# The first six pairs' steps in another order, with GpSimd at work from the first load on

## The chip, the cores and the metric

One Trainium2 chip, one of its cores. The metric is device time in microseconds (us) of one execution. The kernel before took 942.79 us (median of 3 runs, 941.56 to 943.15). The profile comes from one more execution of 941.53 us, whose instructions span 939.8 us. A difference of under 0.2% (about 1.9 us) can't be told from none here.

## The reference

Attention over 8 batches of 8 heads (576 tokens, 64 wide, rotated queries and keys, softmax), whose result goes through a layer of 8 experts, of which each token takes the best one. Cut to what matters:

```python
def rotate(x):
    x1, x2 = (x[..., :half], x[..., half:])
    return np.concatenate([x1 * cos - x2 * sin, x1 * sin + x2 * cos], axis=-1)
q_rot, k_rot = (rotate(q), rotate(k))
scores = scale * np.matmul(q_rot, k_rot.transpose(0, 1, 3, 2))
scores = scores - np.max(scores, axis=-1, keepdims=True)
attn = np.exp(scores)
attn = attn / (np.sum(attn, axis=-1, keepdims=True) + 1e-09)
x = np.matmul(attn, v)            # then, for each token, the expert with the largest logit:
h = np.maximum(xe @ w1[e], 0.0)
out[mask] = gate_w[mask, None] * (h @ w2[e])
```

## The kernel before

The 64 heads are worked on as 32 **pairs** (0 to 31), two heads at a time; the experts follow from about 475 us on. All that the change touches lies in the first 100 us.

A pair is a chain of **steps**, each with a short name: the middle says what it does, the last letter which engine does it (v VectorE, called DVE in the profile; a ScalarE, ACT; g GpSimd, POOL; p TensorE, PE; d a DMA). The steps of pair n:

- FPd fetches queries and keys to a tile `qk` (two such tiles, so the fetch of pair n waits until pair n-2 has been rotated); VPd fetches values.
- RQa, RQc, RQb rotate Q (two products, one sum; `do_R`, lines 561, 563, 566) and RKa, RKc, RKb do it for K. All six read and write SBUF alone, 128x576 in fp32.
- HQ and HK (`do_H`, line 569) round the result to the upper part of a two-part number, LQ and LK (`do_L`, line 581) compute the lower part. Scores are the three products upper x upper, lower x upper, upper x lower.
- DX and DY (`do_D`, line 586) exchange the halves of Q's upper and lower part in SBUF by DMA, so that both heads can be multiplied at once.
- S0 to S8 are the nine score tiles (PE, line 611), M0 to M8 their row maxima (DVE, line 616, from PSUM), E0 to E8 the exponentials (ACT, line 627). Four double banks of PSUM (`pb`) go round: a score tile needs one that an exponential or a copy has freed.
- TA, TB, TR and T3 transpose the exponentials on PE, and cA, cB, cR and c3 copy them out of PSUM (DVE or ACT, line 569). V0 and V1 multiply by the values (line 700), U0 and U1 copy the result, O turns it back (line 742), RZ and X divide by the sums. WT casts a few constants for the routing (four copies on DVE, lines 785 to 788); FL0 to FL4 fill an index list in DRAM.

The order of all this is written by hand in three tables: `FIRST` for the first pairs, then `PLAN`, a window that repeats, then `LAST`. `listed_steps` walks `FIRST` and performs each entry; `chained_emit` ties every instruction of an engine to the one before it on that engine, so the table's order is each engine's order. DMAs are tied on SP's queue alone. `done` keeps a step from being performed twice, so what `FIRST` has done `PLAN` leaves out. Which engine a step runs on is the last letter in the table.

Ahead of the table stand the loads of pair 0 (`first_loads`: Q's half of the tile first, then K's) and `WARM` small matmuls that keep PE at work until the first scores.

## Time and profile before

| | |
|---|---|
| median of 3 runs | 942.79 us |
| the profiled execution, its span | 941.53 us, 939.8 us |
| PE busy over the span | 921.5 us (98%) |
| DVE, ACT, POOL busy | 748.7, 630.1, 653.4 us |
| granted TensorE clock | 1.00 throughout (the level of 2.4 GHz) |

PE is busy nearly all the time, but "busy" is a span from start to modelled end, so a stall shows as little more than a thinner count of matmuls. The share of one engine over the whole span says nothing on the opening: there one reads the stretches (busy time of each engine from one time to another) and the timeline, in which a row gives start, length, engine, line, operation and tiles, and in brackets how long the engine had been idle and who ended that.

### The profile page before, as it was taken

To read this page: it belongs to the slowest core of one execution; us is meant where nothing else is said; L and a number is where in the kernel's file an instruction comes from. 1 tells how busy PE (TensorE), PEld (TensorE's weight loads), DVE (VectorE), ACT (ScalarE), POOL (GpSimd) and SP (SyncE) were. 2 spreads that over 40 slices of the span, in tenths; PEclk is the share of its full clock that TensorE was granted. 3 is DMA by queue.
4 is the path that set the end of the run, shared out by engine and by line. 5 is a ranking of instruction groups with operands and counts; after the bars stand their busy time and mean duration, and the time that the engine had idled before them with its cause. 6 is when DMAs were issued, how large, how long until landed. Compare 5 with 4: busy or idle time off the path is not lost.

```text
span 939.8 us, 25385 instructions
## 1 busy us (share of the span) xinstructions
PE 921.5 (98%) x9579; PEld 769.7 (82%) x9579; DVE 748.7 (80%) x1305; ACT 630.1 (67%) x1123; POOL 653.4 (70%) x559
## 2 busy tenths in 40 slices
...
GB/s 263 244 255 171 168 165 151 187 180 147 184 175 203 133 209 157 129 167 106 220 75 48 72 225 234 206 51 123 163 56 155 157 51 47 44 168 194 409 352 52
...
## 3 DMA queue, kind: packets, MB, share of 16 engines
...
q8 instruction: 77, 1.26, 0.6%
q14 instruction: 56, 0.45, 0.2%
...
## 4 chain that ended last, share of the span: by engine, by line
issue 21%; POOL 18%; PE 10%; DMA 2%; POOLq 1%; DVE 0%; SPq 0%; ACT 0%; DVEq 0%; ACTq 0%
POOL xg L447 6%; POOL xt L447 6%; PE pb L1184 5%; POOL out_dram L1210 4%; PE pb L1320 3%; POOL xsm L1070 1%; DMA out_dram<-y,gi 1%; POOLq L1253 1%; PE pb L700 1%; DMA r<-in_moe_w_dram 1%; DMA xg<-x_dram,gi 0%; PE pb L1133 0%; POOLq L447 0%; DVE PT L569 0%; POOLq L1210 0%
## 5 line engine op out<-in xcount | busy, mean ns | idle before, releaser
L627 ACT ACTIVATE pn<-pb,negm 128x576 f32<-128x576 f32 x256 | 187.4, 739 | 60.1 <-DVE negm L616 57.6
L616 DVE TENSOR_REDUCE negm<-pb 128x1 f32<-128x576 f32 x288 | 201.3, 746 | 23.2 <-PE pb L611 19.0
L611 PE MATMUL pb<-rK,rX 64*128 64x288 f32 (+1 forms) x960 | 163.9, 307 | 3.4 <-ACT pn L627 0.9
L611 PE MATMUL pb<-rK,rQ 64*128 64x288 f32 (+1 forms) x960 | 163.8, 307 | 2.8 <-DVE PT L569 1.0
L1184 PE MATMUL pb<-xh,w1h 128*128 128x256 f32 x544 | 153.8, 283 | 0.0
L1184 PE MATMUL pb<-xh,w1l 128*128 128x256 f32 x544 | 153.7, 283 | 0.0
L1184 PE MATMUL pb<-xl,w1h 128*128 128x256 f32 x544 | 153.7, 283 | 0.0
L700 PE MATMUL pb<-PT,vn 128*64 128x320 f32 (+1 forms) x1024 | 148.9, 412 | 1.0 <-ACT pn L627 0.5
L611 PEld LDWEIGHTS pb<-rK,rX 64*128 64x128 f32 (+1 forms) x960 | 131.9, 179 | 21.6 <-issue 9.8
L611 PEld LDWEIGHTS pb<-rK,rQ 64*128 64x128 f32 (+1 forms) x960 | 131.6, 179 | 11.3 <-DVE PT L569 7.4
L447 POOL DMA_INDIRECT xg<-x_dram,gp x64 | 91.5, 1430 | 54.7 <-DVE gp L257 38.2
L1089 DVE TENSOR_TENSOR w2l<-r,w2h 128x1024 fp32r<-128x1024 f32 x89 | 107.3, 1216 | 19.5 <-ACT w2h L1088 17.3
L569 ACT COPY PT<-pb 128x1024 f32<-128x1024 f32 (+1 forms) x112 | 101.7, 930 | 26.1 <-PE pb L661 22.1
L447 POOL DMA_INDIRECT xt<-x_dram,gp x56 | 80.8, 1442 | 49.1 <-DVE gp L257 31.7
L700 PEld LDWEIGHTS pb<-PT,vn 128*64 128x64 f32 x1024 | 67.9, 136 | 49.7 <-issue 5.7
L1184 PEld LDWEIGHTS pb<-xh,w1h 128*128 128x128 f32 x544 | 106.1, 195 | 0.7
L1184 PEld LDWEIGHTS pb<-xh,w1l 128*128 128x128 f32 x544 | 106.1, 195 | 0.5
L1089 DVE TENSOR_TENSOR w1l<-r,w1h 128x1024 fp32r<-128x1024 f32 x88 | 104.5, 1219 | 2.2 <-ACT w1h L1088 1.8
L1320 PE MATMUL pb<-w2h,hh 128*128 128x512 f32 x272 | 106.2, 390 | 0.0
L1184 PEld LDWEIGHTS pb<-xl,w1h 128*128 128x128 f32 x544 | 106.1, 195 | 0.0
L1320 PE MATMUL pb<-w2l,hh 128*128 128x512 f32 x272 | 106.0, 390 | 0.0
L1320 PE MATMUL pb<-w2h,hl 128*128 128x512 f32 x272 | 105.9, 389 | 0.0
...
## 6 DMA issues: line engine op xcount, KB each, us to landing
...
rX<-rQ SPq DMA_DIRECT2D x128, 144.0 KB
...
```

Source lines behind the costliest of these rows:

```text
L447: nc.gpsimd.indirect_dma_start(out=t[:, k], out_offset=None, in_=x_dram.rearrange("n (q w) -> (n q) w", q=4), in_offset=bass.IndirectOffse ...
L569: (nc.scalar.copy if eng == "a" else nc.vector.tensor_copy)(out=o, in_=i)
L611: nc.tensor.matmul(sp[0:m, r, 0:HS], lhsT=st["Q" if r == h else "X"][rows[r], a, cols], rhs=parts(st["K"][rows[r], b])[:, h], start=(a + b ...
L616: nc.vector.tensor_reduce(out=st["negm"][:, j:j + 1], in_=st["S", j][:, :, 0:HS], axis=AX.XY, op=ALU.max, negate=True)
L627: nc.scalar.activation(out=parts(pt), in_=sp[:, :, 0:HS], func=AF.Exp, bias=st["negm"][:, j:j + 1], scale=1.0, accum_out=z)
L700: m = nc.tensor.matmul(to[:, 0:w], lhsT=st["vn"][:, h, kt, :], rhs=st["PT"][:, 4 * h + kt, half * 256:half * 256 + w], start=(kt == 0), st ...
L1070: nc.gpsimd.indirect_dma_start(out=xsm[:, j], out_offset=None, in_=x_dram, in_offset=bass.IndirectOffsetOnAxis(ap=sib[:, j:j + 1], axis=0) ...
L1089: nc.vector.tensor_tensor(out=lo, in0=src, in1=hi.bitcast(F32), op=ALU.subtract)
L1184: m = nc.tensor.matmul(hp[:, fi], lhsT=w, rhs=x, start=(i == 0), stop=(i == len(todo) - 1))
L1210: sc = nc.gpsimd.indirect_dma_start(out=out, out_offset=bass.IndirectOffsetOnAxis(ap=si[:, t:t + 1], axis=0), in_=y, in_offset=None, bound ...
L1253: nc.gpsimd.drain()
L1320: m = nc.tensor.matmul(yp[:, t], lhsT=h[:, fi, ts_], rhs=w[:, fi], start=(g == 0 and fi == 0 and i == 0), stop=(g == FQ - 1 and fi == 1 an ...
```

## The change

Three edits. The part of `FIRST` up to pair 6 is written in another order and with other engine letters; from pair 3's gate on (`gBv` 3) every engine's order is as before. `WARM` falls from 195 to 185. In `do_D`, pair 0's first half of each exchange is issued from ACT's queue and not SP's. The first two lines of the table, before and after, and the other edits:

```diff
-    ("RQav", 0), ("FPd", 1), ("RQcv", 0), ("RQbv", 0), ("HQa", 0), ("DXd", 0), ("WIa", 0), ("RKcv", 0), ("LQv", 0),
-    ("DYd", 0), ("RKav", 0), ("RKbv", 0), ("RKav", 1), ("RQav", 1), ("HKa", 0), ("FPd", 2), ("RQag", 2), ("RQcv",
+    ("RKcg", 0), ("FPd", 1), ("RQav", 0), ("RQcv", 0), ("RQbv", 0), ("HQa", 0), ("DXd", 0), ("RKav", 0), ("RQcg",
+    1), ("LQv", 0), ("RKbv", 0), ("HKa", 0), ("WIa", 0), ("RKcv", 1), ("DYd", 0), ("RQav", 1), ("LKv", 0), ("RQbv",
...
-WARM = 195
+WARM = 185
...
         for h in range(2):
-            m = nc.sync.dma_start(out=st["X"].bitcast(F32)[rows[1 - h], a], in_=st["Q"].bitcast(F32)[rows[h], a])
+            q = nc.sync if n or h else nc.scalar
+            m = q.dma_start(out=st["X"].bitcast(F32)[rows[1 - h], a], in_=st["Q"].bitcast(F32)[rows[h], a])
```

**Steps that change engine.** From VectorE to GpSimd: RKc 0, RQc 1, RKa 1, RKc 2. From GpSimd to VectorE: RKc 3, LK 3, RKa 4, RQb 4, RKc 4, LK 4, RQb 5, LK 5. Casts from ScalarE to VectorE: HQ 3, HQ 4, HK 4, HQ 5, HK 7. Copies from VectorE to ScalarE: cA0 2, cA0 3, U0 3, U1 3, cB1 5; the other way: cA1 5. WT moves from pair 4's scores to pair 3's.

**The opening on VectorE.** Before, from the first rotation to the first maximum (`qk_138` is pair 0's tile, `qk_347` pair 1's; `yQ`, `yK` are rotated, `rQ`, `rK` the two-part tiles):

```order
L561 TENSOR_TENSOR qk_138<-qk_138,rotq_112 128x576
L563 TENSOR_TENSOR qk_138<-qk_138,rotq_112 128x576
L566 TENSOR_TENSOR yQ_350<-qk_138 128x576
L563 TENSOR_TENSOR qk_138<-qk_138,rotk_111 128x576
L581 TENSOR_TENSOR rQ_353<-yQ_350,rQ_353 128x576
L561 TENSOR_TENSOR qk_138<-qk_138,rotk_111 128x576
L566 TENSOR_TENSOR yK_365<-qk_138 128x576
L561 TENSOR_TENSOR qk_347<-qk_347,rotk_111 128x576
L561 TENSOR_TENSOR qk_347<-qk_347,rotq_112 128x576
L563 TENSOR_TENSOR qk_347<-qk_347,rotq_112 128x576
L563 TENSOR_TENSOR qk_347<-qk_347,rotk_111 128x576
L566 TENSOR_TENSOR yQ_381<-qk_347 128x576
```

Behind these come LK 0, RKb 1 and the first maximum, so fourteen steps stand ahead of it. Now, to the first maximum (the tiles' numbers are new: `qk_337` is pair 1's):

```order
L561 TENSOR_TENSOR qk_138<-qk_138,rotq_112 128x576
L563 TENSOR_TENSOR qk_138<-qk_138,rotq_112 128x576
L566 TENSOR_TENSOR yQ_341<-qk_138 128x576
L561 TENSOR_TENSOR qk_138<-qk_138,rotk_111 128x576
L581 TENSOR_TENSOR rQ_344<-yQ_341,rQ_344 128x576
L566 TENSOR_TENSOR yK_352<-qk_138 128x576
L563 TENSOR_TENSOR qk_337<-qk_337,rotk_111 128x576
L561 TENSOR_TENSOR qk_337<-qk_337,rotq_112 128x576
L581 TENSOR_TENSOR rK_343<-yK_352,rK_343 128x576
L566 TENSOR_TENSOR yQ_362<-qk_337 128x576
L566 TENSOR_TENSOR yK_381<-qk_337 128x576
L617 TENSOR_REDUCE negm_374<-pb0_104 128x1
```

Eleven steps are left on VectorE. The other three open GpSimd's queue now (the first three rows; the fourth is LQ 1, then pair 2 begins), where before its first step was RQa of pair 2:

```order
L563 TENSOR_TENSOR qk_138<-qk_138,rotk_111 128x576
L563 TENSOR_TENSOR qk_337<-qk_337,rotq_112 128x576
L561 TENSOR_TENSOR qk_337<-qk_337,rotk_111 128x576
L581 TENSOR_TENSOR rQ_366<-yQ_362,rQ_366 128x576
L563 TENSOR_TENSOR qk_369<-qk_369,rotq_112 128x576
```

The sixth and the last row on VectorE, RKb of pairs 0 and 1, need the first and the third of these.

**VectorE in pair 2's scores.** Before, from M0 2 on: maxima, the reciprocal sums of pairs 0 and 2 (RZ), U1 0, two copies.

```order
L616 TENSOR_REDUCE negm_760<-pb2_106 128x1
L734 TENSOR_REDUCE rz_857<-z0_124 128x10
L735 RECIPROCAL rz_857<-rz_857 128x10
L616 TENSOR_REDUCE negm_760<-pb0_104 128x1
L616 TENSOR_REDUCE negm_760<-pb1_105 128x1
L616 TENSOR_REDUCE negm_760<-pb2_106 128x1
L734 TENSOR_REDUCE rz_889<-z2_128 128x10
L735 RECIPROCAL rz_889<-rz_889 128x10
L720 COPY uT0_130<-pb3_107 128x5x64
L569 COPY PT_931<-pb0_104 128x2x2x256
```

Now the same stretch has HQ 3, LK 3, RKa 4, RQb 4, RKc 4 and HQ 4 among the maxima (`qk_715` is pair 4's tile):

```order
L569 CAST rQ_803<-yQ_784 128x576
L617 TENSOR_REDUCE negm_753<-pb2_106 128x1
L735 TENSOR_REDUCE rz_820<-z0_124 128x10
L736 RECIPROCAL rz_820<-rz_820 128x10
L581 TENSOR_TENSOR rK_802<-yK_750,rK_802 128x576
L561 TENSOR_TENSOR qk_715<-qk_715,rotk_111 128x576
L617 TENSOR_REDUCE negm_753<-pb0_104 128x1
L566 TENSOR_TENSOR yQ_871<-qk_715 128x576
L617 TENSOR_REDUCE negm_753<-pb1_105 128x1
L617 TENSOR_REDUCE negm_753<-pb2_106 128x1
L563 TENSOR_TENSOR qk_715<-qk_715,rotk_111 128x576
L721 COPY uT0_130<-pb3_107 128x5x64
```

HQ 4 follows these rows; RKc 3 stands a little ahead of them, among pair 1's copies.

## Rows read from the trace of the kernel before

**Rows 1.** Stretches: from:to, length, busy (instructions) of PE, PEld, DVE, ACT, POOL, clock

```profile
13.37:20.00 6.63, 4.48 (x50) 3.37 (x48) 6.44 (x11) 4.38 (x11) 1.74 (x2) 1.00 0.99 308
20.00:40.00 20.00, 17.19 (x278) 13.55 (x276) 19.21 (x26) 18.81 (x42) 19.45 (x14) 1.00 0.73 221
40.00:60.00 20.00, 19.86 (x260) 14.48 (x260) 14.89 (x28) 16.84 (x40) 19.84 (x16) 1.00 0.87 274
60.00:80.00 20.00, 19.62 (x318) 15.45 (x316) 18.73 (x26) 14.77 (x31) 18.79 (x14) 1.00 0.54 158
200.00:300.00 100.00, 99.53 (x1452) 76.00 (x1450) 81.44 (x151) 78.50 (x169) 90.93 (x81) 1.00 0.62 174
```

**Rows 2.** Timeline of VectorE: first two rotations, and the first maxima

```profile
6.28 0.76 DVE L561 TENSOR_TENSOR qk<-qk,rotq 128x576 f32<-128x576 f32 x1 [5.28 <-DMA qk<-in_qk_dram]
6.95 0.75 DVE L563 TENSOR_TENSOR qk<-qk,rotq 128x576 f32<-128x576 f32 x1
...
11.38 0.75 DVE L561 TENSOR_TENSOR qk<-qk,rotk 128x576 f32<-128x576 f32 x1
...
16.18 3.41 DVE L616 TENSOR_REDUCE negm<-pb 128x1 f32<-128x576 f32 x5
```

**Rows 3.** Timeline of the other engines in the opening

```profile
1.06 12.38 PE L990 MATMUL pb<-onesb 128*128 128x128 bf16 x195 [1.06 <-DVE onesb L224]
...
15.53 0.40 PE L611 MATMUL pb<-rK,rX 64*128 64x288 f32 x1 [0.90 <-DVE rK L581]
...
9.23 3.09 SPq L586 DMA_DIRECT2D rX<-rQ  x4
...
16.96 0.74 ACT L627 ACTIVATE pn<-pb,negm 128x576 f32<-128x576 f32 x1
...
22.70 0.78 ACT L627 ACTIVATE pn<-pb,negm 128x576 f32<-128x576 f32 x1
```

**Rows 4.** Timeline of GpSimd from its first step, and VectorE's one step beside it

```profile
18.26 1.42 POOL L561 TENSOR_TENSOR qk<-qk,rotq 128x576 f32<-128x576 f32 x1 [16.29 <-DVE negm L616]
...
23.88 1.41 POOL L581 TENSOR_TENSOR rK<-yK,rK 128x576 fp32r<-128x576 f32 x1
25.25 1.93 POOL L581 TENSOR_TENSOR rQ<-yQ,rQ 128x576 fp32r<-128x576 f32 x1
...
24.02 1.88 DVE L563 TENSOR_TENSOR qk<-qk,rotk 128x576 f32<-128x576 f32 x1
```

**Rows 5.** Timeline of VectorE: other SBUF steps, and GpSimd beside two of them

```profile
69.13 1.02 DVE L785 CAST tid<-cst 128x640 int32<-128x640 f32 x1
70.07 1.39 DVE L786 COPY run<-cst 128x8 f32<-128x8 f32 x1
...
72.80 2.07 DVE L616 TENSOR_REDUCE negm<-pb 128x1 f32<-128x576 f32 x3
...
69.76 1.67 POOL L566 TENSOR_TENSOR yQ<-qk 128x576 f32<-128x576 f32 x1
...
434.90 0.45 DVE L569 CAST rQ<-yQ 128x576 fp32r<-128x576 f32 x1
```

**Rows 6.** Timeline of VectorE from 35 us: its idle times, and c3 of three pairs

```profile
35.81 1.23 DVE L569 COPY PT<-pb 128x1024 f32<-128x1024 f32 x1 [0.61 <-PE pb L661]
...
43.15 2.09 DVE L616 TENSOR_REDUCE negm<-pb 128x1 f32<-128x576 f32 x3 [1.76 <-PE pb L611]
46.25 0.17 DVE L734 TENSOR_REDUCE rz<-z 128x10 f32<-128x20 f32 x1 [1.01 <-ACT pn L627]
...
51.67 0.46 DVE L569 COPY PT<-pb 64x64 f32<-64x64 f32 x2
...
53.26 0.76 DVE L616 TENSOR_REDUCE negm<-pb 128x1 f32<-128x576 f32 x1
...
65.54 0.46 DVE L569 COPY PT<-pb 64x64 f32<-64x64 f32 x2
...
80.03 0.46 DVE L569 COPY PT<-pb 64x64 f32<-64x64 f32 x2
```

22 lines of the change are left out of this document (7 added, 15 removed), and 68 rows, old and new, of the table FIRST.

## The prediction

> **What bounds the kernel now.** I read the stretches first [rows 1]. From 40 us on TensorE is busy nearly without a break (99.5% of 200 to 300 us), and a pair takes 13.87 us from one c3 to the next (51.67 to 65.54) [rows 6]. Ahead of 40 us it is not: 2.15 us idle of the 6.63 to 20 us, 2.81 us to 40 us, while from 20 to 40 us VectorE is busy for 19.21 us, GpSimd for 19.45 and ScalarE for 18.81 of 20 us. So the opening hangs on the engines that feed TensorE, and what it loses there is never given back, since TensorE bounds what follows. The most that a better order of this stretch can bring is about those 5 us; what a worse one costs has no such limit.
>
> Then I read the opening itself. VectorE rotates two pairs alone, from 6.28 us, when Q has landed, to the first maximum at 16.18 us, 0.67 us from one step to the next [rows 2]. GpSimd begins at 18.26 us [rows 4]. TensorE's warming matmuls end at 13.44 us, its last wait for VectorE's lower part of K at 15.53 us, and nine exponentials begin from 16.96 to 22.70 us, one each 0.72 us [rows 3]. Next I looked for what VectorE and GpSimd do when both work on SBUF, since the change makes them do so all along. At 24.02 us VectorE has its one rotation beside GpSimd, RKc 2: 1.88 us for a step of 0.75 [rows 4]. The reader is to see three ends there: GpSimd's step of 23.88 us ends unhurt at 25.29, VectorE's 0.61 us later at 25.90, and GpSimd's next, which began at 25.25, only at 27.18, 1.28 us after VectorE's. The two did not overlap; they took turns. A copy of eight columns (`run`, 70.07 us) takes 1.39 us in the same way, until GpSimd's step of 69.76 ends, and that step itself is stretched to 1.67 [rows 5]. A cast to fp32r with GpSimd at rest takes 0.45 us.
>
> **The opening, step by step.** The change takes three of fourteen steps ahead of the first maximum from VectorE and gives them to GpSimd, and VectorE needs their results ahead of its sixth, tenth and eleventh. If the two take turns, the time is the sum: 11 x 0.67 = 7.4 us and 3 x 1.28 = 3.8 us behind 6.28 us, which makes the first maximum 17.5 us, 1.3 us later than now. If they worked side by side, GpSimd's second and third step could begin when pair 1 has landed (it has by 11.38 us, when VectorE reads it without a wait [rows 2]) and end 2 x 1.41 us later, at 14.2 us, and RKb 1 would end at 14.9 us: 1.3 us earlier than now. These are the bounds, and I take the first, since RKc 2 at 24.02 us is the same operation beside the same operation.
>
> The other two edits cost and bring nothing in that case. Ten warming matmuls fewer are 10 x 12.38 / 195 = 0.63 us, so TensorE is free at 12.8 us, but the upper part of K is then there only after six steps of VectorE, one or two of GpSimd and a cast: 6.28 + 4.0 + 2.6 + 0.7 = 13.6 us at the later end, and its lower part only after nine and three, 6.28 + 6.0 + 3.8 = 16.1 us, against 15.5 now. The exchange on two queues takes two of four issues of 0.77 us (3.09 / 4 [rows 3]) off SP, so the lower half of Q goes about 1.5 us earlier; the wait for the lower part of K ends after it in either order, so that hides it. On ScalarE's queue the two issues stand ahead of the cast of K. If each holds that engine as long as one holds SP's queue, 0.77 us, the second, which waits for LQ 0 (five steps and one, 6.28 + 3.4 + 1.3 = 11.0 us), is through at 11.8, ahead of that cast, which waits for RKb 0: nothing. Cover gone, it would be 0.8 us.
>
> **VectorE up to pair 0's output.** From its first maximum (16.18 us) to the first one behind pair 0's X (53.26 us) VectorE takes 37.1 us, of which it idles 0.61 + 1.76 + 1.01 = 3.4 us [rows 6]: 33.7 us of work. The change takes RKc 2 with its stall (1.88) and the copy cA0 2 (1.23) away: 30.6. It adds RKc 3, LK 3, RKa 4, RQb 4, RKc 4, 5 x 0.67, and the casts HQ 3 and HQ 4, 2 x 0.45: 34.8 us. That is without a turn waited for. Each of the seven waits between nothing (GpSimd at rest) and 1.28 us. GpSimd is busy for 39.3 of the 40 us from 20 to 60 us now [rows 1], but in the new order it often waits for one of these very steps (LQ 3 for HQ 3, RKb 4 for RKa 4 and RKc 4, LQ 4 for HQ 4), so I take 0.45 us each, a third: 3.1 us. Of the 3.4 us of idling most is filled; I keep 0.8. Sum: 17.5 + 34.8 + 3.1 + 0.8 = 56.2 us against 53.26: **+2.9 us**. What is late next are pair 2's last maxima: exponentials, transposes and so TensorE wait for them, and only four double banks of PSUM lie between.
>
> **The pair behind it.** From c3 of pair 1 to that of pair 2 VectorE now also has WT, which takes from 69.13 to 72.80 us, 3.7 us, for waiting in turn [rows 5]; before, it lay one pair later, and that pair took 14.49 us (65.54 to 80.03) and not 13.87 [rows 6]. The new sum: nine maxima 6.2 (3.41 / 5 each), WT 3.7, LK 4 and RQb 5 1.3, HK 4 and HQ 5 0.9, two copies of U at most 0.9 together (c3, of two small copies, is 0.46), one of PT 1.2, c3 and X 1.6 (51.67 to 53.26): 15.8 us, and turns of some 0.1 us net, since WT's price holds GpSimd fully busy and here it has six steps of 1.41 in that time. I take 15.9: 2.0 over the 13.87 of before, and the pair after it falls from 14.49 to 13.87: **+1.4 us**. Behind that only LK 5 and HK 7 are added, some 2 us in two pairs in which VectorE has to spare (it is busy 81.44 of 100 us later on [rows 1]), and from pair 3's gate on the order is the old one.
>
> **Sum:** +2.9 + 1.4 = +4.3 us on an execution of 941.53 us, 945.8; the median of the runs lies 1.26 us above the profiled one, so 947.1. Ends of this case: with hardly a turn waited for and no idling, 17.5 + 34.8 + 0.5 = 52.8, and WT at 2.5 us, it comes to about 0, which is the first rival; with half a turn for each of the seven and the four steps and 1.5 us of idling, 17.5 + 34.8 + 4.5 + 1.5 - 53.3 = 5.0 and 15.8 + 2.6 - 13.9 - 0.6 = 3.9, so +8.9.
>
> **The rivals.** *The added steps fall into GpSimd's rests.* GpSimd begins 10 us earlier, has four steps fewer up to pair 3's gate, and waits for VectorE at four places. Then only the opening's 1.3 us is lost and RKc 2's stall of 1.1 us is won back: between -1.9 and +1.9 us, about +0.3, 943.1 us. For it: `uT`, maxima and copies from PSUM lie between most of the added steps. Against it: three of them follow each other within two maxima.
>
> *The two engines do work side by side, and the change is faster.* The place is the opening. The first maximum comes at 14.9 us, the exponentials with it, RKc 2 is gone from VectorE, and up to pair 0's output it ends at 14.9 + 34.8 + 1.2 idle = 50.9 us, 2.4 us earlier; WT then lies in a pair that TensorE bounds, 0.6 us more: -3.0 us, 939.8 us. It decides from the point where VectorE's mean wait per rotation beside GpSimd is under about 0.2 us. For it speaks that RKc 2 is a single row of its kind; against it, that its three ends fit taking turns to 0.1 us, and the copies in rows 5. The Trainium skill's page "Advanced Engine Details and Errata" (VectorE Performance Modes, Mode Summary) names blocking by GpSimd only for VectorE's two-port modes, and "VectorE: DVE Perf Modes" has none of those for an fp32 tensor_tensor: by these two alone the rotations would run free and this rival would be the forecast. The row at 24.02 us differs, and "SBUF — State Buffer" (SBUF: two separate sides) has the wider rule, a lock against any step with two SBUF inputs, which the row bears out; so the measurement decides for turns.
>
> *TensorE's clock falls.* It is granted 1.00 in all stretches, through waits to 15.53 us too. In the new opening TensorE stands nearly idle from 12.8 to 16.1 us. An estimate from the warming matmuls, which run at the upper level (2.4 GHz): 128 columns take 0.063 us [rows 3], 288 columns 0.143, and a pair's nine score tiles, 30 double steps, 4.3 us; at the lower level (1.2 GHz) 8.6 us, against 9 x 0.72 = 6.5 us of exponentials, which hide the first and not the second: +2.1 us more. I count it, at one in ten, within the forecast.
>
> That the table is not followed is no rival: the built order has the three steps at the head of GpSimd's queue.
>
> **How the numbers follow.** Under 0.2% (1.9 us) can't be told from none. The forecast (turns, VectorE late in pairs 2 and 3, +1.9 to +9 us) 0.58; the rests 0.21; side by side 0.21. So slower 0.58, same 0.21, faster 0.21. The range leaves about a tenth on either side: 940.0 takes in half of the faster case, 951.5 most of the turns.
>
> **What would show it.** Right: in the opening VectorE's rotations from the fourth on alternate between 0.75 and some 2 us, the first maximum stands at 17.5 us, SBUF steps among pair 2's maxima take over 1 us each, TensorE's count of matmuls from 40 to 60 us falls, and c3 of pair 1 comes some 3 us later. Wrong: rotations of 0.75 us beside GpSimd's of 1.41, a first maximum ahead of 16 us, and c3 of pair 2 ahead of 65 us.

## The result and the profile after

The changed kernel is slower: 951.67 us (median of 4 runs, 951.09 to 952.16) against 942.96 for the kernel before beside it (941.56 to 943.15), a ratio of 1.0095, 95% interval 1.0078 to 1.0113. That is +8.7 us; +4.3 were forecast, with a range to 951.5 us. The profiled execution took 951.09 us (span 949.3), 9.6 us more than the profiled one of before. Behind the first edits the lines of the code are one higher than before.

The opening, VectorE's timeline and GpSimd's (start, length, engine, line, operation, tiles, and in brackets the idle time ahead and who ended it); it answers to [rows 2] and [rows 4]:

```profile
6.19 0.76 DVE L561 TENSOR_TENSOR qk<-qk,rotq 128x576 f32<-128x576 f32 x1 [5.19 <-DMA qk<-in_qk_dram]
...
8.32 1.96 DVE L561 TENSOR_TENSOR qk<-qk,rotk 128x576 f32<-128x576 f32 x1
10.21 0.75 DVE L581 TENSOR_TENSOR rQ<-yQ,rQ 128x576 fp32r<-128x576 f32 x1
10.88 1.96 DVE L566 TENSOR_TENSOR yK<-qk 128x576 f32<-128x576 f32 x1
12.75 1.96 DVE L563 TENSOR_TENSOR qk<-qk,rotk 128x576 f32<-128x576 f32 x1
...
17.31 2.08 DVE L617 TENSOR_REDUCE negm<-pb 128x1 f32<-128x576 f32 x3
```

```profile
7.78 1.89 POOL L563 TENSOR_TENSOR qk<-qk,rotk 128x576 f32<-128x576 f32 x1 [5.80 <-DMA qk<-in_qk_dram]
10.67 1.55 POOL L563 TENSOR_TENSOR qk<-qk,rotq 128x576 f32<-128x576 f32 x1 [1.00 <-DMA qk<-in_qk_dram]
12.18 1.92 POOL L561 TENSOR_TENSOR qk<-qk,rotk 128x576 f32<-128x576 f32 x1
```

Three of VectorE's rotations take 1.96 us and the others 0.75, each of the three beside one of GpSimd's three steps. The engines take turns, and the first maximum comes at 17.31 us (16.18 before).

The stretches, which answer to [rows 1] (from:to, length, busy time and instructions of PE, PEld, DVE, ACT, POOL, then the granted clock):

```profile
20.00:40.00 20.00, 17.80 (x288) 14.14 (x284) 18.61 (x27) 18.84 (x44) 18.68 (x14) 1.00 0.96 247
40.00:60.00 20.00, 17.78 (x228) 13.77 (x228) 19.48 (x30) 13.25 (x30) 12.35 (x9) 0.91 0.68 196
48.00:50.00 2.00, 0.71 (x16) 0.58 (x16) 2.00 (x4) 0.83 (x3) 0.00 (x0) 1.00 0.56 167
50.00:52.00 2.00, 1.69 (x40) 1.55 (x40) 2.00 (x3) 2.00 (x6) 1.39 (x1) 0.86 0.00 0
52.00:54.00 2.00, 2.00 (x26) 2.00 (x26) 1.97 (x5) 1.79 (x2) 1.55 (x3) 0.50 0.27 58
54.00:56.00 2.00, 2.00 (x34) 2.00 (x32) 1.81 (x3) 1.54 (x5) 2.00 (x2) 0.79 0.88 176
470.00:480.00 10.00, 8.15 (x76) 5.40 (x72) 3.54 (x5) 3.21 (x7) 6.17 (x3) 0.83 0.80 290
```

From 40 to 60 us VectorE is busy for 19.48 us, where it was for 14.89, and GpSimd for 12.35, where it was for 19.84: the work has gone from one to the other. TensorE is busy for 0.71 of the 2 us from 48 to 50 us, and behind that its granted clock falls from 1.00 to 0.50 (the level of 1.2 GHz) for some 3.4 us: (0.14 + 0.50 + 0.21) x 2 / 0.5. It falls again at 474 us. The first fall hardly sets a time, since VectorE is the late one there; what it idles is 0.41 us, ahead of X (below).

VectorE from the first of its seven added steps to X of pair 0, with pair 2's maxima among them, and ScalarE, which waits for these:

```profile
35.22 1.47 DVE L563 TENSOR_TENSOR qk<-qk,rotk 128x576 f32<-128x576 f32 x1
...
41.07 1.34 DVE L569 CAST rQ<-yQ 128x576 fp32r<-128x576 f32 x1
...
43.32 1.25 DVE L581 TENSOR_TENSOR rK<-yK,rK 128x576 fp32r<-128x576 f32 x1
44.49 1.96 DVE L561 TENSOR_TENSOR qk<-qk,rotk 128x576 f32<-128x576 f32 x1
46.38 0.74 DVE L617 TENSOR_REDUCE negm<-pb 128x1 f32<-128x576 f32 x1
47.04 1.43 DVE L566 TENSOR_TENSOR yQ<-qk 128x576 f32<-128x576 f32 x1
48.39 1.41 DVE L617 TENSOR_REDUCE negm<-pb 128x1 f32<-128x576 f32 x2
49.72 0.74 DVE L563 TENSOR_TENSOR qk<-qk,rotk 128x576 f32<-128x576 f32 x1
...
50.79 1.54 DVE L569 CAST rQ<-yQ 128x576 fp32r<-128x576 f32 x1
...
56.22 0.82 DVE L767 TENSOR_TENSOR xt<-pb,rz 128x640 f32<-128x640 f32 x1 [0.41 <-PE pb L674]
56.96 0.23 DVE L769 TENSOR_TENSOR lgt<-pb,rz 128x80 f32<-128x80 f32 x1
```

```profile
47.16 0.74 ACT L628 ACTIVATE pn<-pb,negm 128x576 f32<-128x576 f32 x1 [3.21 <-DVE negm L617]
...
49.17 0.74 ACT L628 ACTIVATE pn<-pb,negm 128x576 f32<-128x576 f32 x1 [1.18 <-DVE negm L617]
```

The row at 56.96 us ends X of pair 0. In the kernel before it is

```profile
52.88 0.23 DVE L768 TENSOR_TENSOR lgt<-pb,rz 128x80 f32<-128x80 f32 x1
```

Such a row stands in every kernel for each of the 32 pairs, and its distance to the same row of the kernel before is called the **lateness** of that pair's X here: +4.1 us for pair 0, +5.1 for pair 1, +5.1 for pair 3, +5.8 for pair 9, +7.2 for pair 29 and +9.6 for pair 30, behind the start of the experts. So half of the loss arises up to X of pair 1, and nearly all of the other half behind pair 3.

### The profile page after: what moved, and what is told of

Read it like the earlier page. It is cut to its first block, busy times and chain, and to the rows that moved or that the text cites. A ratio compares the mean times of both kernels' runs of the same rounds, so it can differ in the third digit from the quotient of the medians.

```text
span 949.3 us, 25373 instructions
## 1 busy us (share of the span) xinstructions
PE 926.8 (98%) x9569; PEld 773.1 (81%) x9569; DVE 756.7 (80%) x1310; ACT 630.3 (66%) x1122; POOL 648.7 (68%) x555
## 4 chain that ended last, share of the span: by engine, by line
PE 42%; issue 21%; POOL 17%; DMA 7%; DVE 7%; ACT 2%; POOLq 1%; SPq 1%; DVEq 0%; ACTq 0%
PE pb L612 10%; PE pb L701 10%; PE pb L1185 7%; PE pb L1321 6%; POOL xg L447 5%; POOL xt L447 4%; PE pb L638 4%; POOL out_dram L1211 4%; DVE PT L569 3%; PE pb L743 3%; PE pb L706 2%; DMA qk<-in_qk_dram 2%; DVE negm L617 1%; ACT pn L628 1%; DMA out_dram<-y,gi 1%
## 5 line engine op out<-in xcount | busy, mean ns | idle before, releaser
L612 PE MATMUL pb<-rK,rX 64*128 64x288 f32 (+1 forms) x960 | 166.2, 309 | 4.7 <-ACT pn L628 1.9
L612 PE MATMUL pb<-rK,rQ 64*128 64x288 f32 (+1 forms) x960 | 166.2, 309 | 3.3 <-DVE lgt L769 1.4
```

What stands on the lines that cost most here:

```text
L612: nc.tensor.matmul(sp[0:m, r, 0:HS], lhsT=st["Q" if r == h else "X"][rows[r], a, cols], rhs=parts(st["K"][rows[r], b])[:, h], start=(a + b ...
```

## The experiments

Medians are in us, each beside the kernel before on the same chip. Lateness is that of the profiled execution, in us.

| kernel | median, before | ratio, 95% interval | X 0 | X 1 | X 3 | X 9 | X 29 | X 30 |
|---|---|---|---|---|---|---|---|---|
| changed kernel | 951.7, 943.0 | 1.0078 to 1.0113 | +4.1 | +5.1 | +5.1 | +5.8 | +7.2 | +9.6 |
| late_start | 947.1, 943.1 | 1.0026 to 1.0054 | +3.7 | +3.7 | +3.3 | +3.5 | +4.3 | +4.7 |
| small_edits | 942.9, 943.1 | 0.9987 to 1.0017 | -1.1 | -1.1 | -1.7 | -2.2 | -1.6 | -1.6 |
| open_on_vector | 952.7, 943.1 | 1.0069 to 1.0130 | +3.9 | +5.7 | +7.0 | +6.9 | +7.6 | +7.7 |
| back_to_gpsimd | 953.6, 943.1 | 1.0070 to 1.0140 | +3.4 | +5.6 | +8.7 | +8.5 | +9.2 | +11.2 |
| changed_again | 949.9, 943.7 | 1.0050 to 1.0099 | +3.3 | +4.5 | +4.8 | +5.2 | +5.8 | +8.2 |
| clock_held | 952.1, 943.7 | 1.0055 to 1.0108 | +4.9 | +8.7 | +8.7 | +9.1 | +10.2 | +10.3 |
| maxima_first | 950.9, 943.7 | 1.0058 to 1.0098 | +2.9 | +4.1 | +6.8 | +7.1 | +7.9 | +8.2 |
| open_shared | 950.4, 943.7 | 1.0056 to 1.0102 | +7.0 | +7.0 | +6.9 | +7.6 | +8.9 | +8.9 |
| new_opening | 943.8, 942.8 | 1.0000 to 1.0020 | +0.7 | +0.7 | +1.2 | +1.7 | +1.7 | +1.5 |
| old_opening | 947.2, 942.8 | 1.0033 to 1.0066 | +3.3 | +4.5 | +7.3 | +7.5 | +8.2 | +8.3 |
| pair4_late | 953.0, 942.8 | 1.0081 to 1.0131 | +2.5 | +4.9 | +6.6 | +9.4 | +10.4 | +10.9 |
| order_alone | 949.1, 942.9 | 1.0029 to 1.0080 | +3.9 | +5.1 | +7.5 | +8.3 | +8.9 | +10.7 |
| engines_alone | 952.8, 942.9 | 1.0069 to 1.0127 | +5.6 | +9.6 | +11.5 | +12.6 | +12.7 | +12.4 |
| hk7_on_scalar | 950.9, 942.9 | 1.0054 to 1.0114 | +2.3 | +6.3 | +6.5 | +8.9 | +9.6 | +11.3 |
| rkc2_on_gpsimd | 942.9, 942.9 | 0.9989 to 1.0019 | +0.8 | +0.8 | +0.2 | +0.3 | +0.3 | +0.3 |
| loads_early | 950.9, 942.9 | 1.0039 to 1.0093 | +2.9 | +7.3 | +7.0 | +7.5 | +8.2 | +12.1 |
| loads_early_changed | 951.1, 942.9 | 1.0047 to 1.0093 | +3.4 | +6.4 | +6.1 | +6.3 | +7.0 | +9.5 |

Single executions of one kernel differ by up to 5 us and more where the clock falls in some and not in others, so the medians tell only differences of some 3 us, and lateness tells which place loses. Lateness is that of one execution too: the changed kernel's two profiles (changed kernel, changed_again) differ by 0.8 us at X 0 and by 1.4 at X 29.

### Is a late start carried to the end?

**late_start**, against the kernel before: only TensorE begins later.

```diff
-WARM = 195
+WARM = 310
```

> The kernel before with 310 warming matmuls for 195: nothing but TensorE's start is late. At 0.063 us each they end at 1.06 + 310 x 0.0635 = 20.7 us, so the first maximum comes at about 21.2 us, 5.0 us behind that of before (16.18). Theory (what is lost ahead of 55 us is carried to the end one for one, and what the changed kernel lost behind 60 us is due to its order): +5 us, some 948 us, and the distance to the kernel before stays the same from pair 1 to the end. Rival (to be late is enough: the waits for the expert gather, the second fall of the clock behind them and the slow drift come with any late start): +7 to +9 us, some 951 us, with a clock below 1.00 near the transition. A third outcome: under +3 us, if VectorE and GpSimd, which go ahead meanwhile, win part of it back.

The first maximum came at 21.26 us, 5.1 us late. By pair 0's X 3.7 were left, since VectorE and GpSimd had gone ahead meanwhile, and that stood within 0.4 us to pair 24 and within 0.7 to pair 29; the median is 4.0 us over. So from X 0 on TensorE does carry a delay one for one, and lateness alone doesn't bring 9.6 out of 4.1. Some of the growth comes with any kernel, since the execution of before that the rows are from (941.53 us) lies 1.3 to 2.2 us under the medians of that kernel.

### The small edits

**small_edits**, against the kernel before:

```diff
-WARM = 195
+WARM = 185
...
-            m = nc.sync.dma_start(out=st["X"]
+            q = nc.sync if n or h else nc.scalar
+            m = q.dma_start(out=st["X"]
```

> The kernel before with the two small edits alone: 185 warming matmuls for 195, and pair 0's exchange of Q's halves on two queues; its order of steps is the old one. Theory (the prediction's: both hidden): within 1 us of the kernel before, 942 to 943.5 us, first maximum between 15.5 and 16.3 us. Rival (ScalarE's two issues delay the cast of K, and so the first scores): first maximum at 17 us, some +0.8 us. Rival two (the wait for the lower part of K ends on those transfers): first maximum up to 0.8 us earlier, and the time with it.

First maximum at 16.10 us, the time that of before: nothing, as forecast. In its profile RKc 2 took 0.97 us instead of 1.88, because GpSimd's first step came 1.0 us earlier (17.25 us for 18.26): the load of pair 2 was issued 1.0 us earlier (11.41 for 12.45), since two of pair 0's exchanges stood ahead of it on SP's queue and not four. X 0 was 1.1 us early there. What a turn costs hangs on such shifts.

### The opening apart

**open_on_vector**, against the changed kernel:

```diff
-("RKcg", 0) ... ("RQcg", 1) ... ("RKag", 1)
+("RKcv", 0) ... ("RQcv", 1) ... ("RKav", 1)
```

> The changed kernel with the three opening steps that it gave GpSimd (RKc 0, RQc 1, RKa 1) on VectorE. Theory (the two engines take turns, so GpSimd's part in the opening only costs): fourteen steps of 0.67 us behind 6.28 us, first maximum at about 16.1 us and not 17.3, and the time 1 to 2 us below that of the changed kernel, some 950 us; pair 2's late maxima stay, and the clock falls behind them all the same. Rival (GpSimd's early share gives it the lead that it needs later): the first maximum is as early, yet the time stays at 951 to 952 us. Rival two (the fall of the clock hangs on little): with 1.2 us more in hand the clock stays at 1.00 and the time is 3 us or more lower.

This said little: RKc 0 stands first in the changed order, so VectorE waited for K, which lands 1.6 us behind Q, and the first maximum was no earlier (17.47 us, where 16.1 were expected). It tells something else: its profile was granted 1.00 from end to end, and yet its last X are 7.7 us late.

The mirror image, **open_shared**, against the kernel before: the three steps on GpSimd, in the order of before.

```diff
-("RKcv", 0) ... ("RKav", 1) ... ("RQcv", 1)
+("RKcg", 0) ... ("RKag", 1) ... ("RQcg", 1)
```

> The kernel before with three of the opening's fourteen steps (RKc 0, RQc 1, RKa 1) on GpSimd, in the places that its own order has them. Theory (the engines take turns, so GpSimd's steps of 1.28 us beyond VectorE's are added): VectorE's steps beside them take 1.9 us, the first maximum comes at 17.5 us or later, and the time is 1 to 2 us over that of before. Rival (three steps fewer on VectorE let it end earlier): first maximum at 15 us, time 1 us under before. Rival two (the exchanges of K's halves, which hang on those steps, come late): first maximum at 18 us or later, +2 us or more.

Rival two in its times, but not by its reason (exchanges that come late), and by one that I hadn't seen: in that order pair 2's first step stands ahead of RQc 1 in GpSimd's queue and waits for a load, VectorE waits for RQc 1, and TensorE for the K behind it. VectorE and GpSimd:

```profile
21.55 0.76 DVE L565 TENSOR_TENSOR yQ<-qk 128x576 f32<-128x576 f32 x1 [7.07 <-POOL qk L562]
...
18.77 1.40 POOL L560 TENSOR_TENSOR qk<-qk,rotq 128x576 f32<-128x576 f32 x1 [6.24 <-DMA qk<-in_qk_dram]
20.12 1.40 POOL L562 TENSOR_TENSOR qk<-qk,rotq 128x576 f32<-128x576 f32 x1
```

First maximum at 23.68 us, 7.5 late; all later X are 6.9 to 8.9 late. The two together led to the clean cut, each half of the change with the other half of before (the two small edits stand in the second alone):

**new_opening**, against the kernel before: `FIRST` of the changed kernel up to ("S8p", 0), then all steps that are left in the order and on the engines of before.

```diff
-FIRST = [ ("RQav", 0), ("FPd", 1), ("RQcv", 0), ("RQbv", 0), ("HQa", 0),
+FIRST = [ ("RKcg", 0), ("FPd", 1), ("RQav", 0), ("RQcv", 0), ("RQbv", 0),
...
+("FPd", 2), ("VPd", 0), ("RQag", 2), ("VPd", 1), ("LQg", 1), ("RQcg", 2), ("RQbg", 2), ("S8p", 0), ("RKbv", 1),
```

> The other half: the kernel before with the changed opening, up to the first score tile, and all that stands behind in the old order with its engines. Theory (the opening costs 1.1 to 1.3 us at the first maximum, and that is carried one for one): first maximum at 17.4 us, every later X 1.1 to 1.3 us behind, 944 to 944.5 us. Rival (GpSimd's lead of three steps is worth more than that, since in the old order it is busy without a break from 20 to 60 us): the first X no later than before, 942 us or less, which would beat both. Rival two (the clock falls behind TensorE's wait at 14 to 16 us): another 1.7 us or more, 946 us.

**old_opening**, against the changed kernel: `FIRST` of before up to ("S8p", 0), then all steps that are left in the changed order on the changed engines.

```diff
-FIRST = [ ("RKcg", 0), ("FPd", 1), ("RQav", 0), ("RQcv", 0), ("RQbv", 0),
+FIRST = [ ("RQav", 0), ("FPd", 1), ("RQcv", 0), ("RQbv", 0), ("HQa", 0),
...
+("RQcg", 2), ("RQbg", 2), ("LKv", 0), ("S8p", 0), ("RKbv", 1), ("S5p", 0), ("S1p", 0),
```

> The changed kernel with the opening's steps, up to the first score tile, in the old order and on the old engines (14 rotations on VectorE, GpSimd begins with pair 2), and all that stands behind in the changed order with its engines. Theory (VectorE's added steps and turns behind the first maximum cost most, the opening 1.1 us): first maximum at 16.2 us, the first X still 2.5 to 4 us behind that of the kernel before, the time 1 us under the changed kernel's, some 950 us. Rival (the changed order lives on the lead that GpSimd has from the opening): the first X 5 us or more behind, 952 us or more. Rival two (the opening is what costs): the first X less than 1.5 us behind, 945 us.

The opening alone costs 1.0 us (0 to 1.9): first maximum at 17.46 us, 1.3 late, as the turns have it. In its profile the clock fell from 19.1 to 22.6 us, the place of the second rival, and X 0 was 0.7 us late all the same: that fall cost nothing which shows there. The rest alone costs 4.4 us (3.1 to 6.2), with the first maximum at 16.26 us and a clock of 1.00 to 97 us, and its X 0 is as late as in the changed kernel's second profile (+3.3 both). So most of the loss lies behind the first maximum, and up to 97 us it isn't the clock's.

### Pair 2's maxima

**back_to_gpsimd**, against the changed kernel: eight rotations and lower parts back on GpSimd, the order kept.

```diff
-("RKcv", 3) ("LKv", 3) ("RKav", 4) ("RQbv", 4) ("RKcv", 4) ("LKv", 4) ("RQbv", 5) ("LKv", 5)
+("RKcg", 3) ("LKg", 3) ("RKag", 4) ("RQbg", 4) ("RKcg", 4) ("LKg", 4) ("RQbg", 5) ("LKg", 5)
```

> The changed kernel with eight rotations and casts-to-lengths of pairs 3, 4 and 5 (RKc 3, LK 3, RKa 4, RQb 4, RKc 4, LK 4, RQb 5, LK 5) back on GpSimd, in the places where the changed order has them. Theory (VectorE's added steps and its turns with GpSimd made pair 2's maxima late, TensorE idle at 46 to 50 us and its clock fall behind that): the first maximum behind pair 0's X comes at 54.5 us or earlier, the clock stays at 1.00 from 50 to 56 us, and the time is 943 to 946 us, 6 us or more below the changed kernel's. Rival (GpSimd, which now has eight steps more, becomes the one that is late, so that the scores of pairs 3 and 4 wait for it): 950 us or more, with TensorE's waits for the DMA of rotated keys and queries in the 45 to 75 us stretch. Rival two (the order itself, not the engine, makes it late): no difference to the changed kernel, 951 to 952 us.

The first rival. Pair 2's last three maxima were nearly in time (43.87 us, 43.15 before), but the cast HQ 4, left on VectorE, now waits there for GpSimd, and the copy behind it for which TensorE waits comes late:

```profile
49.64 1.66 DVE L569 CAST rQ<-yQ 128x576 fp32r<-128x576 f32 x1 [1.27 <-POOL yQ L566]
...
51.55 1.17 DVE L569 COPY PT<-pb 128x1024 f32<-128x1024 f32 x1
...
52.77 0.40 PE L612 MATMUL pb<-rK,rQ 64*128 64x288 f32 x1 [1.61 <-DVE PT L569]
```

Later HK 7, also left on VectorE, waits 3.28 us for GpSimd, and X 3 is 3.3 us later than X 2.

**maxima_first**, against the changed kernel: two of the steps behind the maxima, no engine changed.

```diff
-("RKav", 4), ("S8p", 2) ... ("M8v", 2) ... ("RQbv", 4), ("M7v", 2) ... ("M5v", 2), ("E7a", 2), ("RKcv", 4)
+("S8p", 2) ... ("M8v", 2) ... ("M7v", 2) ... ("M5v", 2), ("E7a", 2), ("RKav", 4), ("RQbv", 4), ("RKcv", 4)
```

> The changed kernel with two of VectorE's added steps (RKa 4, RQb 4; 1.96 and 1.43 us with their turns) moved behind the last three maxima of pair 2, ahead of which they stood; nothing else is moved, and no step changes its engine. Theory (what costs is the place: two steps that nobody needs yet stand in VectorE's queue ahead of maxima that ScalarE and TensorE wait for): ScalarE's waits of 3.21 and 1.18 us at 44 to 49 us shrink to under 1 us in all, TensorE's transposes of pair 2 come 2 to 3 us earlier, the clock stays at 1.00, the first X comes 1.5 us or less behind that of the kernel before, and the time is 3 to 5 us under the changed kernel's, 947 to 949 us. Rival (VectorE has too much work up to there, wherever it stands): the same lateness comes out at X or at the pair behind, and the time stays within 1.5 us of the changed kernel's.

The last three maxima came earlier (44.77 us for 46.38), the clock stayed at 1.00 there (it fell at 17.8 and 96.4 us), and X 0 was 1.2 us less late than in the first profile of the changed kernel, 0.4 less than in the second. But the copies behind the moved steps came late instead, and the median is 1.0 us over the changed kernel's on this chip (949.9): the rival. TensorE's waits at 24 to 76 us (engine, tile, line, for whom; us in total, times, longest):

```profile
PE pb L610 <- DVE PT L567: 2.4, 3, 1.2
```

**pair4_late**, against the changed kernel: four steps and what hangs on them moved, two of them behind X 0.

```diff
-("LQg", 3), ("RKav", 4) ... ("V1p", 0), ("RQbv", 4) ... ("E7a", 2), ("RKcv", 4) ... ("U0a", 0), ("HQv", 4), ("RKbg", 4)
+("cB1v", 2), ("RQbv", 4) ... ("M0v", 3), ("HQv", 4), ("LQg", 4), ("DXd", 4) ... ("Xv", 0), ("RKav", 4) ... ("c3v", 1), ("RKcv", 4), ("RKbg", 4)
```

> The changed kernel with the four steps of pair 4 that it put ahead of pair 0's X on VectorE, and what hangs on them, moved later: RQb 4 behind the last PT copy that pair 2's scores need, HQ 4 behind pair 3's first maxima, RKa 4 and RKc 4 behind pair 0's X; no step changes its engine. Theory (VectorE has too much work ahead of pair 0's X, and the order put there what nobody needs yet): pair 2's maxima no longer late, the clock at 1.00 from 48 to 56 us, the first X 1 to 1.5 us behind that of before, and the time 3 us or more under the changed kernel's, 946 to 948 us. Rival (what is moved is missed in the pair behind): the first X is early, but the second or third falls back, and the time stays at 950 us or more.

The rival again: X 0 is less late than in the changed kernel (+2.5 us), X 1 as late as ever (+4.9), X 3 and X 4 more (+6.6, +9.7): VectorE's cast HK 7 waits 3.42 us for GpSimd, which the steps put off have held up.

### The clock

**changed_again** is the changed kernel once more, with no edit.

> The changed kernel once more, as it is, beside the next three on the same chip. Theory A (the two falls of the clock are part of what the change brings, each 3.4 us at half clock, since TensorE idles at 46 to 50 us and at 472 to 474 us in every execution): 951 to 953 us, clock under 1.00 at 50 to 56 us and at 472 to 480 us again. Theory B (they are chance): in one profile or the other place the clock stays at 1.00, and the time is lower by 1.7 us for each fall that is missing.

Both theories hold in part. Behind the near idle stretch at 48 to 50 us (1.06 us busy of 2) the clock stayed at 1.00 this time; at 473 us it fell again. And it fell in the opening, where the prediction had looked for it, from 16.1 to 22.9 us: TensorE had stood from 14.3 to 16.3 us.

```profile
14.00:16.00 2.00, 0.28 (x4) 0.04 (x2) 2.00 (x3) 0.40 (x1) 0.26 (x1) 1.00 0.83 281
16.00:18.00 2.00, 1.73 (x14) 1.74 (x16) 2.00 (x4) 1.09 (x2) 0.33 (x1) 0.52 1.06 323
```

Pair 0's ninth maximum came 1.0 us later for that (23.85 us for 22.87), but X 0 did not: +3.3 us with this fall, +4.1 in the profile without it.

**clock_held**, against the changed kernel: TensorE kept busy in two places.

```diff
+    def hold(ps, k):
+        for _ in range(k):
+            nc.tensor.matmul(ps[:, 0, 0:P], lhsT=onesb, rhs=onesb, start=True, stop=True)
...
+        if n == 2:
+            hold(tp, 20)
...
+        if s == 0:
+            hold(ps, 32)
```

For pair 2 that is 8 ahead of TA 0, 20 ahead of TR and 4 ahead of TB 1, and 32 ahead of the first expert's transposes, each into a tile that is then overwritten.

> The changed kernel with TensorE kept busy where it idled: 8, 20 and 4 matmuls like the warming ones (0.063 us each) ahead of pair 2's transposes, into the tile that these then overwrite, and 32 ahead of the first expert's transposes. Theory (of the 9 us, 3.4 are two falls of the clock, 1.7 us each, and the rest is lateness of VectorE's maxima that TensorE waits for): clock 1.00 in both places, the first X at 2.4 us behind the kernel before and not 4.1, the experts 3 us earlier than in the changed kernel: 948 to 949 us. Rival (the lateness alone costs, since TensorE would have waited anyway for what it ran slowly through): 951 to 952 us with the clock at 1.00.

Held in both places: 1.00 from 46 to 60 us, and at the start of the experts, where the filling matmuls took 1.96 us, X 30 is 0.1 us later than X 29, not 2.4. The rest of the theory failed. X 0 is 4.9 us late, where 2.4 were expected: the clock had fallen in the opening (18.7 us), and the five maxima that begin at 37.74 us in the changed kernel began at 39.58, ahead of the first filling matmul. So this run doesn't show what the fall at 51 us costs. And the execution lost 3.7 us more between X 0 and X 1. VectorE came to WT 1.0 us later than in the changed kernel, when GpSimd's load had landed and it was at work again (60.93 us), and two small copies took 1.40 and 1.39 us, as [rows 5] had it, where the changed kernel's took 0.16 each (its first of the two, then both of clock_held):

```profile
59.99 0.16 DVE L787 COPY run<-cst 128x8 f32<-128x8 f32 x1
...
60.97 1.40 DVE L795 COPY run<-cst 128x8 f32<-128x8 f32 x1
...
62.42 1.39 DVE L797 COPY rk<-cst 128x5 f32<-128x5 f32 x1
```

The stretches behind that:

```profile
66.00:68.00 2.00, 1.17 (x30) 0.89 (x28) 2.00 (x4) 1.80 (x5) 1.03 (x1) 1.00 1.01 354
68.00:70.00 2.00, 1.31 (x40) 1.18 (x39) 2.00 (x4) 1.57 (x2) 0.48 (x2) 0.98 0.03 8
70.00:72.00 2.00, 2.00 (x22) 2.00 (x20) 1.71 (x3) 1.04 (x2) 2.00 (x2) 0.50 0.52 121
```

Pair 3's maxima came late, TensorE was idle for 1.5 of the 4 us from 66 us, and the clock fell there instead. To fill the waits at two places did not rid this execution of the falls.

### Order or engines?

The part behind the opening, divided once more.

**order_alone**, against old_opening: the changed order, every step on its engine of before.

```diff
-("RKcg", 2) ("RKcv", 3) ("HQv", 3) ("LKv", 3) ("RKav", 4) ("RQbv", 4) ("RKcv", 4) ("HQv", 4) ("cA0a", 2) ("HKv", 4)
+("RKcv", 2) ("RKcg", 3) ("HQa", 3) ("LKg", 3) ("RKag", 4) ("RQbg", 4) ("RKcg", 4) ("HQa", 4) ("cA0v", 2) ("HKa", 4)
-("LKv", 4) ("RQbv", 5) ("cA0a", 3) ("HQv", 5) ("LKv", 5) ("U0a", 3) ("HKv", 7) ("U1a", 3) ("cB1a", 5) ("cA1v", 5)
+("LKg", 4) ("RQbg", 5) ("cA0v", 3) ("HQa", 5) ("LKg", 5) ("U0v", 3) ("HKa", 7) ("U1v", 3) ("cB1v", 5) ("cA1a", 5)
```

> The changed order behind the first score tile, with the opening of before and every step on the engine that it has in the kernel before. Theory (what costs is the work that VectorE was given, with its turns and its waits for GpSimd): the first X less than 1.5 us behind that of before, 943 to 944.5 us. Rival (the order costs, on whichever engine): the first X some 3 us behind, pair 1 one more, 947 us, as with the changed engines in that order (947.2).

**engines_alone**, against the kernel before: the same letters the other way round, in the order of before.

```diff
-("RKcv", 2) ("RKcg", 3) ("RKcg", 4) ("HQa", 3) ("RQbg", 4) ("LKg", 3) ("HQa", 4)
+("RKcg", 2) ("RKcv", 3) ("RKcv", 4) ("HQv", 3) ("RQbv", 4) ("LKv", 3) ("HQv", 4)
...
```

> The counterpart: the kernel before in its own order, with the engines of the changed kernel for all steps behind the first score tile (eight rotations and five casts more on VectorE, RKc 2 on GpSimd, four copies exchanged). Theory (the engines cost): the first X 3 us or more behind that of before, 946 to 948 us. Rival (the order costs): within 1.5 us of the kernel before, 943 to 944.5 us. Should both halves be dear, each 945 us or more, the two add up, and neither alone is the cause; should both be cheap, it is their meeting.

Both are dear, +6.3 us (2.7 to 7.5) and +10.0 (6.5 to 12.0), and together (old_opening) they cost 4.4 (3.1 to 6.2): less than the engines alone, and no more than the order alone, as far as the intervals tell. So they don't add up, though the expectation had them do so, and neither is the cause by itself: an order fits its engines. Of the changed engines in the old order GpSimd's timeline shows a part of why:

```profile
52.71 1.42 POOL L579 TENSOR_TENSOR rQ<-yQ,rQ 128x576 fp32r<-128x576 f32 x1 [4.81 <-DVE rQ L567]
...
59.54 1.41 POOL L564 TENSOR_TENSOR yK<-qk 128x576 f32<-128x576 f32 x1 [5.41 <-DVE qk L559]
```

It stands 10 us for steps that VectorE has not come to.

### GpSimd's rests

The changed kernel's GpSimd, and VectorE's cast HK 7:

```profile
60.46 1.56 POOL L563 TENSOR_TENSOR qk<-qk,rotq 128x576 f32<-128x576 f32 x1 [3.84 <-DMA qk<-in_qk_dram]
...
77.47 1.41 POOL L561 TENSOR_TENSOR qk<-qk,rotk 128x576 f32<-128x576 f32 x1 [5.54 <-DMA qk<-in_qk_dram]
...
93.40 1.66 DVE L569 CAST rK<-yK 128x576 fp32r<-128x576 f32 x1 [1.65 <-POOL yK L566]
```

It rests 3.84 and 5.54 us for the loads of pairs 6 and 7, and later VectorE waits for it, with two copies queued behind that TensorE needs. In old_opening that wait is 3.02 us and costs X 3 3.0 us. **hk7_on_scalar**, against old_opening: that cast alone moved back.

```diff
-("HKv", 7)
+("HKa", 7)
```

> The changed kernel with the opening of before (947.2 us when it ran), and in it one more step as it was before: the cast HK 7 on ScalarE. Theory (VectorE stands 3.0 us in its queue at 91 to 94 us for GpSimd's part of that cast, with two copies behind it for which TensorE waits 2.4 us): TensorE's wait at 94 to 97 us falls to under 0.5 us, X of pair 3 comes as far behind as X of pair 2 (4.3 us, not 7.3), and the time is 2 to 3 us lower, 944.5 to 945.5 us. Rival (the cast waits on ScalarE too, ahead of exponentials and copies that TensorE needs): the same wait with another releaser, 947 us.

The wait at pair 3 went, as the theory has it (X 3 only 0.3 us later than X 2), yet the time didn't fall. Ahead of the moved cast this execution had already lost more than old_opening's (X 1 +6.3 us, not +4.5): WT stood beside a GpSimd at work and took 4.2 us, not 0.7. The clock fell four times, and GpSimd, still late, was waited for at pair 5:

```profile
127.57 0.58 PE L610 MATMUL pb<-rK,rQ 64*128 64x288 f32 x1 [1.87 <-POOL rK L579]
```

So the two loads were moved ahead, in old_opening (**loads_early**) and in the changed kernel (**loads_early_changed**):

```diff
-("M3v", 3), ("FPd", 6) ... ("E6a", 4), ("FPd", 7)
+("cB1v", 2), ("FPd", 6) ... ("FL0d", 0), ("FPd", 7)
```

> The changed kernel with the opening of before (947.2 us when it ran), and in it the loads of pairs 6 and 7 further ahead in the queue of transfers: that of pair 6 ahead of pair 4's exchange, for which the queue waits to 52.4 us, that of pair 7 ahead of pair 5's, for which it waits to 67.6. No step is moved on another engine. Theory (GpSimd's rests for these loads, 3.3 and 6.4 us, make its part of HK 7 late, and VectorE and TensorE with it): the rests fall to under 1.5 us each, VectorE's wait of 3.0 us at 91 to 94 us goes, X of pair 3 is no further behind than X of pair 2, 944.5 to 946 us. Rival (GpSimd, busy now where it rested, takes turns with VectorE's four small copies of WT, 3.1 us instead of 0.7, and with more steps): pair 1's X 2 us later, and the time the same, 947 us or more.

> The same two loads moved in the changed kernel as it is, with its own opening. Theory: GpSimd's rests of 3.84 and 5.54 us fall to under 1.5 us each, what the profile shows as lost behind pair 1 up to pair 9 (0.7 us) goes, and the waits at pair 3; 1 to 2.5 us under the changed kernel's 950 to 951.7 us. Rival (WT's turns): pair 1's X 2 us later, 951 us or more. Rival two (the rests were harmless, since GpSimd was ahead): no change.

Theory and rival both came true in the main, and cancel. In loads_early the rests fell to 2.13 and 1.38 us, VectorE's wait for HK 7 to 1.30 (not to nothing), and X 3 is no later than X 2; in loads_early_changed the rests fell to 1.99 and 1.81 us and the wait to 1.32. But WT now runs beside a GpSimd that works. It takes 3.9 and 3.8 us, and X 1 is 4.5 us later than X 0 in loads_early (2.9 to 7.3), where it was 1.1, and 3.0 in loads_early_changed. First VectorE in loads_early, then GpSimd:

```profile
58.55 1.28 DVE L784 CAST tid<-cst 128x640 int32<-128x640 f32 x1
59.75 1.39 DVE L785 COPY run<-cst 128x8 f32<-128x8 f32 x1
...
61.19 1.37 DVE L787 COPY rk<-cst 128x5 f32<-128x5 f32 x1
...
58.06 1.41 POOL L561 TENSOR_TENSOR qk<-qk,rotq 128x576 f32<-128x576 f32 x1 [2.13 <-DMA qk<-in_qk_dram]
...
74.29 1.41 POOL L559 TENSOR_TENSOR qk<-qk,rotk 128x576 f32<-128x576 f32 x1 [1.38 <-DMA qk<-in_qk_dram]
```

Either GpSimd works, and VectorE's small steps wait for it, or it rests, and is late itself.

### The one part that could help

**rkc2_on_gpsimd**, against the kernel before:

```diff
-("RKcv", 2)
+("RKcg", 2)
```

> The kernel before with RKc 2, VectorE's one rotation beside GpSimd (1.88 us at 24.02 us), on GpSimd: nothing else. Theory (turns: VectorE wins 1.2 to 1.9 us there, GpSimd loses 1.4 less the 0.5 us that the turn stretched its own step): the first X 0.3 to 1 us earlier, 942 to 942.8 us, under what the measurement can tell from nothing. Rival (GpSimd is the fuller engine from 20 to 60 us, so 0.9 us more there comes out at the rotated keys of pairs 3 and 4): the first or second X 1 us later, 944 us.

As the theory has it, no difference; GpSimd's loss eats VectorE's gain. No kernel here beats the one before.

## Where the prediction was right, and the step that failed

**What bounds.** Right in the main: TensorE bounds what follows, and what is still late at X 0 isn't given back; late_start and open_shared show it with the order untouched. But not all that the opening loses gets that far: of late_start's 5.1 us 3.7 were left at X 0, of new_opening's 1.3 us 0.7.

**The opening.** Right in mechanism and size: turns, with the first maximum at 17.31 us (17.5 forecast), and +1.0 us (0 to 1.9) when made alone. The rival in which the engines work side by side is out, and so is that of GpSimd's rests. The Trainium skill's page "SBUF — State Buffer" (SBUF: two separate sides) has a lock between the two engines: the rows agree, with 1.96 us for a step of 0.75. The Trainium skill's page "Perfetto Trace Analysis" (Optimizing Scalar/DVE Operations) warns that moving operations between the two might not help: new_opening agrees, +1.0 us for three steps moved. The two small edits at nothing: right (small_edits).

**VectorE up to X 0.** The mechanism was right, the term too small. The forecast was seven turns at 0.45 us, 3.1 us, and 0.8 us of idling. In the profile the seven steps take 1.47, 1.25, 1.96, 1.43, 0.74, 1.34 and 1.54 us against 0.75 (five) and 0.45 (two) at rest: 9.7 - 4.65 = 5.1 us of turns, 0.73 each, and VectorE idles 1.6 us. With the forecast's 34.8 us of work that makes 17.3 + 34.8 + 5.1 + 1.6 = 58.8 us; measured are 57.59 us for the first maximum behind X 0, so the work was overstated by 1.2 us. Most of that is in the reading of the kernel before: VectorE idles 4.2 us in that stretch and not 3.4, the rest in gaps too short for a bracket, and its cast HK 2 took 0.82 us there in a turn of its own, 0.45 now. Lateness there: +4.3 us where +2.9 were forecast. Six of the seven steps met GpSimd at work, though it was busy for only 12.35 of the 20 us from 40 to 60 us.

**The pair behind.** The size came near (+1.0 us from X 0 to X 1; +1.4 forecast), the reason not: WT cost 0.7 us and not 3.7, since GpSimd happened to rest for a load (3.84 us). So this term came near by luck. Where GpSimd worked, in clock_held and loads_early, WT took 3.2 and 3.9 us, and pair 1 was 3.7 and 4.5 us later than pair 0.

**"Behind that only LK 5 and HK 7 are added."** This is the step that failed: what lies behind the two late pairs was put at nothing, as VectorE's spare time. At c3 of pair 3 (84.93 us, 80.03 before) the profile is 4.9 us late, 0.6 over the forecast; the other 4.7 of its 9.6 come later. Three things stand there. HK 7 was counted as 0.45 us of VectorE's spare time, but it stands in VectorE's queue waiting for GpSimd, with copies behind it: the question that the prediction asked of added waits, who is queued behind, was not asked of this one. It cost X 3 0.2 and 0.5 us in the changed kernel's two profiles and 3.0 in old_opening. Then the start of the experts: there TensorE waits for the first gathered rows (the kernel before, then the changed one),

```profile
466.04 0.98 PE L1133 MATMUL pb<-cst,xg 128*128 128x128 f32 x7 [0.89 <-DMA xg<-x_dram,gi]
...
473.99 1.14 PE L1134 MATMUL pb<-cst,xg 128*128 128x128 f32 x7 [1.85 <-DMA xg<-x_dram,gi]
```

for 1.85 us and not 0.89, and the clock falls behind it: the 24 matmuls that follow take 4.2 us (475.06 to 479.29) and not 2.7 (466.96 to 469.70). X 30 is 2.4 us later than X 29, in both profiles of the changed kernel. Why the gathered rows land later (6.9 and 7.1 us behind GpSimd's issue, 6.1 before) was not followed. And 2.1 us arise bit by bit between pairs 3 and 29, 1.0 in changed_again; late_start, in the old order, shows 1.0 too, so the change need not be the cause of that.

**The clock.** It was a rival at one in ten, placed in the opening, at 2.1 us. It fell there in six of the eight profiles with the changed opening on both engines, so the chance was too low; but the price wasn't borne out: X 0 was 3.3 and 3.4 us late with that fall (changed_again, loads_early_changed) and 4.1 without (the changed kernel's first profile). What cost was its fall at 474 us, where the prediction had not looked. The executions of two kernels part by their mean clock: order_alone took 947.3 to 949.6 us in the five with a mean clock of 0.997 or 0.998, and 952.2 to 952.5 in the three with 0.990 to 0.994; loads_early 946.1 to 950.9 in four with 0.998 or more, 952.0 to 953.7 in three with 0.994 or less. In new_opening they hardly do: 943.7 to 945.0 us in four with 0.993 to 0.995, 942.9 to 944.0 in six with 0.998 or more. So it matters where the clock falls. The changed kernel's eight had 0.995 or 0.996, the kernel before's mostly 0.998 to 1.000. So of the changed kernel's loss some 2 us go with the clock, as an estimate from its profile: 4.2 - 2.7 = 1.5 us at the experts, and at most the 0.41 us that VectorE idled behind the first fall. Most of the loss needs no fall: open_on_vector's profile, at 1.00 throughout, took 949.15 us, 7.6 over the profile of before. That the clock is the cause and not a companion of a longer wait is shown for the start of the experts alone, by one execution (clock_held).

**What stays open.** Opening and rest made alone sum to 5.4 us, the whole to 6.2 and 8.7 on two chips; the intervals overlap, and whether something else comes of their meeting can't be told. Why the changed order with the old engines costs as much as it does was not followed further than to four falls of the clock in its profile, and to ScalarE's copies and a late load of the gate's weights, for which TensorE waited 2.2 and 1.1 us.
